# Attention products on 64-wide tiles of the TensorE array, a pair of heads at a time

## The chip, the cores and the metric

The kernel runs on one core of one Trainium2 chip. A core has a matrix engine (PE, with its weight loads listed apart as PEld), a vector engine (DVE), a scalar engine (ACT), GpSimd (POOL) and SyncE (SP, which here only issues DMAs); they run beside each other and wait for one another through semaphores. PE reads SBUF and writes only PSUM, which has eight banks. The metric is the device time of the whole program in microseconds.

## What is computed

A windowed attention feeds a feed-forward network; all inputs are float32 but for the two weight matrices, which are float64.

```python
B, H, S, D = (8, 8, 576, 64)
scores = q @ k.T / sqrt(D)
mask = (rel >= 0) & (rel < 64)        # rel = query position - key position
attn = softmax(where(mask, scores, -1e9))
x = (attn @ v) as [4608 tokens, 512]
h = x @ w_in                          # 512 -> 2048
sp = where(h > 20, h, log1p(exp(min(h, 20))))
out = (h * tanh(sp)) @ w_out          # 2048 -> 512
```

A query sees itself and the 63 tokens before it, so a block of 64 queries needs two blocks of 64 keys.

## The kernel before

**Tiling.** The 4608 tokens are taken in 12 chunks of 384 (CH), each of 6 blocks of 64 queries (NB). The 8 heads go in 4 pairs (NPAIR); the two heads of a pair fill the 128 partitions, 64 channels each.

**Attention of a chunk.** The work is cut into 8 units of (pair, group of three blocks). Each unit has three stages:

- `att_scores` (L109): for every block one product with 128 rows of contraction, 128 query columns and 128 key columns (L126). The query tile `q_t` comes from `q2`, which the host lays out so that a block has 128 columns, 64 for each head, with zeros in the rows of the other head; so one product gives the scores of both heads. VectorE then scales, masks and takes the row's extreme in one instruction a block (L131), ScalarE takes the exponential with a running sum (L135), VectorE adds 1e-9 and inverts (L137, L138), and the rows are multiplied by the inverse: for chunks 0 to 2 all on GpSimd, later two of three blocks on VectorE (L143) and one on GpSimd (L141).
- `att_transpose` (L146): for chunks 0 and 1 by PE into a PSUM bank and back by ScalarE (L157, L158); from chunk 2 on by 12 VectorE transposes of 32 by 32 squares a unit, over three blocks at a time (L153).
- `att_values` (L161): for every block one product of 128x128 with 128 columns (L165), of which the quarter for (head 0, head 0) and that for (head 1, head 1) are used; ScalarE casts each head's half to the float32r tile `xh` (L172) and VectorE writes the rest to `xl` (L173), two instructions each.

Every float32 product stands in the trace as two pairs of a weight load and a matmul, so 24 products a chunk for scores are 48 pairs, and as many for values.

**Feed-forward.** For each of 16 slices of 128 hidden columns, `ffn_in` (L175) makes h by 12 float32r products (high and low parts, L181), ScalarE, VectorE and GpSimd make the gate's tiles `gh` and `gl` (L188 to L200), and `ffn_out` (L206), two slices later, adds 9 products into three PSUM banks (L211). In stretches without attention beside them, `alone=True` copies h out of PSUM into a tile of the tag `pr` (L191, L192).

**Weights.** `load_w` (L225) splits the doubles into two float32r tiles, 32 pieces in all, four or five VectorE instructions each (L236 to L245), with a scratch tile `wa` of its own (two buffers).

**Order.** First the attention of chunks 0 and 1, with the first eight weight pieces placed behind marked units; then 24 slices of chunks 1 and 0 with two weight pieces after each until they are used up; then the last 8 slices of chunk 0 with the attention of chunk 2 beside them; then for each chunk c from 2 its 16 slices with the attention of chunk c + 1 beside them; the last chunk alone. `Att.plan` (L297) gives every stage a due time in half slices: units start `step` apart, the transpose `lat` later, the values 1.5 `lat` later. The order on each engine is then settled by the compiler's own scheduling within these priorities. The loads of q, k and v all go through SP's queue, two pairs ahead.

**PSUM.** Three banks for the sums (`ps_acc`), two for h (`ps_h`), three for attention (`ps_at`).

Of the kernel before, what the change touches and what calls it, by code (L numbers as in the profile page):

```python
# [11 lines left out]
F32 = mybir.dt.float32  # L12
# [7 lines left out]
BLK = 64          # the attention window; queries and keys go in blocks of it  # L20
# [3 lines left out]
WP = 512          # columns of weights taken at a time  # L24
# [3 lines left out]
def tile_window_attn_mish_ffn(  # L28
    ctx: ExitStack,
    tc: tile.TileContext,  # L30
    q2: bass.AP,      # [pairs, 128 (head of the pair, d), blocks x (head, 64 queries)], zero across heads
    kT: bass.AP,      # [pairs, 128, 64 + tokens]
    vN: bass.AP,      # [pairs, 64 + tokens, 128]
    w_in: bass.AP,    # [f tiles, 128, c tiles, 128], the doubles' bits
    w_out: bass.AP,   # [f tiles, 128, 512], the doubles' bits
    out: bass.AP,     # [tokens, 512]
# [3 lines left out]
    NPAIR, _, NT = q2.shape  # L40
    NT //= 2
# [6 lines left out]
    G = 3                       # blocks of an attention group  # L48
    NG = NB // G
# [16 lines left out]
    mask0 = const.tile([P, P], F32, name="mask0")  # L66
# [7 lines left out]
    nc.gpsimd.tensor_copy(mask0, mask)  # L74
    nc.gpsimd.memset(mask0[:, 0:BLK], NEG)

# [5 lines left out]
    pTs = [const.tile([P, G, P], F32, name=f"pT{i}") for i in range(2)]  # L82
# [4 lines left out]
    marks = {}        # the last of VectorE's instructions on a group's scores  # L87

    def load_qk(c, p):
        q_t = ap_.tile([P, NB, P], F32, name="q_t")  # L90
        k_t = ap_.tile([P, CH + BLK], F32, name="k_t", bufs=2)
        qf = q_t.rearrange("p n s -> p (n s)")
        parts = NG if c == 0 and p < 2 else 1
        for i in range(parts):
            a, b = i * CH // parts, (i + 1) * CH // parts
            nc.sync.dma_start(qf[:, 2 * a:2 * b], q2[p, :, 2 * (c * CH + a):2 * (c * CH + b)])
# [12 lines left out]
    def att_scores(c, i, tiles):  # L109
        p, g = units[i]  # L110
        q_t, k_t = tiles
        if c < 2:
            n = i % NTT
            s_ps = ps_acc.tile([P, G, P], F32, name="s_ps", tag=f"acc{n}")
        else:
            s_ps = ps_at.tile([P, G, P], F32, name="s_ps", tag="at")
        if c < 2 and i % 2 == 0:
            # the tiles of the gate, which has not begun
            pr = mp.tile([P, CH], F32, name="prt", tag="t", bufs=4).rearrange("p (g s) -> p g s", g=G)
        else:  # L120
            pr = ap_.tile([P, G, P], F32, name="pr", bufs=3)
        mx = ap_.tile([P, G], F32, name="mx", bufs=5)
        sm = ap_.tile([P, G], F32, name="sm", bufs=5)
        for j in range(G):
            n = g * G + j
            nc.tensor.matmul(s_ps[:, j, :], q_t[:, n, :], k_t[:, n * BLK:n * BLK + P],  # L126
                             start=True, stop=True)
        for j in range(G):
            first = (c * NB + g * G + j) % blocks_per_seq == 0
            # -(scores + mask) / 8 and its minimum, which is minus the maximum  # L130
            marks[c, i] = nc.vector.tensor_tensor_reduce(  # L131
                out=pr[:, j, :], in0=s_ps[:, j, :], in1=mask0 if first else mask,
                op0=ALU.add, op1=ALU.min, scale=-0.125, scalar=3.0e38, accum_out=mx[:, j:j + 1])
        for j in range(G):
            nc.scalar.activation(pr[:, j, :], pr[:, j, :], AF.Exp, bias=mx[:, j:j + 1], scale=-1.0,  # L135
                                 accum_out=sm[:, j:j + 1])
        nc.vector.tensor_scalar(sm, sm, 1e-9, None, ALU.add)  # L137
        nc.vector.reciprocal(sm, sm)  # L138
        for j in range(G):
            if c < 3 or j == G - 1:  # L140
                nc.gpsimd.tensor_scalar(pr[:, j, :], pr[:, j, :], sm[:, j:j + 1], 0.0, ALU.mult, ALU.add)  # L141
            else:
                nc.vector.tensor_scalar(pr[:, j, :], pr[:, j, :], sm[:, j:j + 1], None, ALU.mult)  # L143
        return pr

    def att_transpose(c, pr):  # L146
        pT = next(pTs)
        if c >= 2:
            # 32 by 32, without the squares that the mask empties
# [5 lines left out]
        t_ps = ps_h.tile([P, G, P], F32, name="t_ps", tag="h_ps")  # L155
        for j in range(G):
            nc.tensor.transpose(t_ps[:, j, :], pr[:, j, :], ident)  # L157
        nc.scalar.copy(pT, t_ps)  # L158
        return pT

    def att_values(p, g, v_t, pT, x):  # L161
        xh, xl = x
        o_ps = ps_at.tile([P, G, P], F32, name="o_ps", tag="at")
        for j in range(G):
            nc.tensor.matmul(o_ps[:, j, :], v_t[:, g * G + j, :], pT[:, j, :], start=True, stop=True)  # L165
        cols = slice(g * G * BLK, (g + 1) * G * BLK)
        for j in range(2):
            rows = slice(j * BLK, (j + 1) * BLK)
            src = o_ps[rows, :, rows]
            hi = xh[rows, p, cols].rearrange("p (n s) -> p n s", s=BLK)  # L170
            lo = xl[rows, p, cols].rearrange("p (n s) -> p n s", s=BLK)
            nc.scalar.copy(hi, src)  # L172
            nc.vector.tensor_tensor(lo, src, hi.bitcast(F32), ALU.subtract)  # L173

    def ffn_in(x, f, alone=False):  # L175
# [7 lines left out]
        t = mp.tile([P, CH], F32, name="t", bufs=4)  # L183
# [13 lines left out]
        # minus h * tanh(softplus(h)); the sign goes at the end  # L197
# [27 lines left out]
    def load_w(src, wh, wl):  # L225
        """Doubles [128, n] as the sum of two float32r tiles, by their bits."""
# [13 lines left out]
        # sign, 8 bits of exponent, 20 bits of the high word and 3 of the low one  # L240
# [18 lines left out]
    # attention of a chunk as a list of (pair, group), each in three stages  # L259
    units = [(p, g) for p in range(NPAIR) for g in range(NG)]  # L260
    NU = len(units)

    class Att:
# [18 lines left out]
        def scores(self, i):  # L282
            p, g = units[i]
            self.pr[i] = att_scores(self.c, i, self.qk[p])
# [130 lines left out]
```

## Time and profile before

| what | value |
|---|---|
| time, median of 3 runs | 1037.87 us (1037.74 to 1038.93) |
| the profiled execution: span of its instructions | 1039.1 us |
| PE busy / weight loads busy | 979.3 us (94%) / 877.7 us (84%) |
| DVE / ACT / POOL busy | 796.2 (77%) / 625.8 (60%) / 398.9 us (38%) |
| chain that ended last, by engine | PE 49%, DVE 34%, ACT 10% |
| HBM read / written | 65.54 / 9.44 MB |

The span is the time from the first to the last instruction of one execution, 1.2 us over the median of the timed runs. A matmul's end is modelled in the trace, so its busy time overlaps that of the next one; the distance from one start to the next is what a matmul costs in a row of them. "Idle before, releaser" names what an engine was waiting for.

### The profile page before, as it was taken

How to read it: one execution, taken by the hardware profiler on the slowest of the kernel's cores; microseconds unless marked ns; L12 is line 12 of the kernel's file. 1: busy time of each engine (PE TensorE's matmuls, PEld its weight loads, DVE VectorE, ACT ScalarE, POOL GpSimd, SP SyncE). 2: the span in 40 equal slices, each digit the busy share in tenths (PEclk: the TensorE clock that was granted, in tenths of full speed). 3: DMA queues.
4: the chain of work that ended last, by engine and by line, in shares of the span. 5: the costliest groups of instructions: out<-in, count | busy, mean ns of one | idle time of the engine just before them, and what ended most of it. 6: DMA issues, size and time to landing. Idle time of an engine off the chain costs nothing.

```text
span 1039.1 us, 16752 instructions
## 1 busy us (share of the span) xinstructions
PE 979.3 (94%) x5232; PEld 877.7 (84%) x5232; DVE 796.2 (77%) x2621; ACT 625.8 (60%) x1668; POOL 398.9 (38%) x583
## 2 busy tenths in 40 slices
PE   7689887977989999999999999999999999999998
PEld 6687776876979988898889898888988889888887
DVE  4899997798778778777787877877877887885332
ACT  6765776555656655665656565655665655655664
POOL 5645555432333332433334233343333333333432
PEclk9889999988999999999999999999999999999999
DMA  8743441232211211211311211221221211200000
GB/s 264 237 136 110 132 124 41 82 93 77 73 55 50 85 55 41 94 51 45 94 41 56 76 58 55 71 64 40 85 64 40 85 42 62 84 3 1 31 1 31
DMA packets 61913, 76.05 MB, mean 73 GB/s; under 512 B 3456, under 2 KB 47232, under 8 KB 61824
## 3 DMA queue, kind: packets, MB, share of 16 engines
q1 hardware_dynamic: 57936, 60.83, 18.8%
q0 software_dynamic: 3888, 14.16, 4.5%
q8 instruction: 41, 0.67, 0.3%
q14 instruction: 48, 0.39, 0.1%
HBM read 65.54 MB, written 9.44 MB: 72 GB/s over the span
## 4 chain that ended last, share of the span: by engine, by line
PE 49%; DVE 34%; ACT 10%; issue 4%; DMA 2%; POOL 1%; SPq 0%; ACTq 0%; DVEq 0%; POOLq 0%
PE h_ps L181 21%; PE acc L211 21%; DVE pT L153 13%; ACT pr L135 4%; PE o_ps L165 3%; PE s_ps L126 3%; DVE t L193 3%; DVE pr L143 3%; DVE t L198 2%; DVE wa L242 2%; DVE xl L173 2%; DVE sm L137 2%; DVE wa L243 2%; ACT t L194 1%; ACT t L195 1%
## 5 line engine op out<-in xcount | busy, mean ns | idle before, releaser
L199 POOL TENSOR_SCALAR gh<-t 128x384 fp32r<-128x384 f32 x192 | 104.1, 542 | 518.9 <-DVE t L198 374.9
L181 PE MATMUL h_ps<-xh,wi_h 128*128 128x384 f32 x768 | 275.3, 359 | 9.4 <-ACT h L192 7.4
L153 DVE STREAM_TRANSPOSE pT<-pr 32x96 f32<-32x96 f32 x960 | 258.4, 269 | 14.3 <-DVE pr L143 0.5
L181 PE MATMUL h_ps<-xl,wi_h 128*128 128x384 f32 x768 | 261.5, 340 | 1.5 <-DVE xl L173 1.4
L181 PE MATMUL h_ps<-xh,wi_l 128*128 128x384 f32 x768 | 260.9, 340 | 0.8 <-POOL wi_l L245 0.8
L194 ACT ACTIVATE t<-t 128x384 f32<-128x384 f32 x192 | 100.8, 525 | 232.3 <-DVE t L193 232.0
L211 PE MATMUL acc<-wo_h,gh 128*128 128x512 f32 x576 | 231.1, 401 | 5.5 <-POOL gh L199 5.5
L211 PE MATMUL acc<-wo_l,gh 128*128 128x512 f32 x576 | 228.0, 396 | 0.0
L211 PE MATMUL acc<-wo_h,gl 128*128 128x512 f32 x576 | 216.4, 396 | 0.0
L200 POOL TENSOR_TENSOR gl<-t,gh 128x384 fp32r<-128x384 f32 x192 | 199.9, 1041 | 15.6
L181 PEld LDWEIGHTS h_ps<-xh,wi_h 128*128 128x128 f32 x768 | 146.9, 191 | 17.9 <-ACT h L192 10.7
L181 PEld LDWEIGHTS h_ps<-xl,wi_h 128*128 128x128 f32 x768 | 147.2, 192 | 4.1 <-DVE xl L173 2.1
L181 PEld LDWEIGHTS h_ps<-xh,wi_l 128*128 128x128 f32 x768 | 146.5, 191 | 2.0 <-POOL wi_l L245 1.5
L198 DVE SCALAR_TENSOR_TENSOR t<-t,h_ps 128x384 f32<-128x384 f32 x152 | 83.8, 551 | 79.7 <-ACT t L196 77.4
L211 PEld LDWEIGHTS acc<-wo_h,gl 128*128 128x128 f32 x576 | 108.0, 188 | 26.6 <-POOL gl L200 1.0
L211 PEld LDWEIGHTS acc<-wo_h,gh 128*128 128x128 f32 x576 | 108.6, 189 | 25.8 <-POOL gh L199 8.3
L211 PEld LDWEIGHTS acc<-wo_l,gh 128*128 128x128 f32 x576 | 108.7, 189 | 17.6
L195 ACT ACTIVATE t<-t,half_b 128x384 f32<-128x384 f32 x192 | 118.3, 617 | 5.2
L135 ACT ACTIVATE pr<-pr,mx 128x128 f32<-128x128 f32 x264 | 102.6, 390 | 25.0 <-DVE mx L131 24.8
L165 PE MATMUL o_ps<-pT,v_t 128*128 128x128 f32 x576 | 92.4, 288 | 25.1 <-DVE pT L153 19.1
L193 DVE TENSOR_SCALAR t<-t 128x384 f32<-128x384 f32 x192 | 95.8, 500 | 25.5 <-ACT t L188 23.7
L165 PEld LDWEIGHTS o_ps<-pT,v_t 128*128 128x128 f32 x576 | 81.0, 198 | 39.1 <-DVE pT L153 18.5
(54 smaller groups left out, 1106.2 us busy)
## 6 DMA issues: line engine op xcount, KB each, us to landing
v_t<-vN SPq DMA_DIRECT2D x48, 384.0 KB, 3.5
q_t<-q SPq DMA_DIRECT2D x46, 384.0 KB, 3.3
k_t<-kT SPq DMA_DIRECT2D x46, 224.0 KB, 3.5
out<-o SPq DMA_DIRECT2D x36, 256.0 KB, 2.1
st<-w_out POOLq DMA_DIRECT2D x14, 512.0 KB, 4.0
st<-w_in POOLq DMA_DIRECT2D x13, 512.0 KB, 4.0
st<-w_in SPq DMA_DIRECT2D x3, 512.0 KB, 5.9
st<-w_out SPq DMA_DIRECT2D x2, 512.0 KB, 4.6
```

Source lines behind the costliest of these rows:

```text
L126: nc.tensor.matmul(s_ps[:, j, :], q_t[:, n, :], k_t[:, n * BLK:n * BLK + P], start=True, stop=True)
L135: nc.scalar.activation(pr[:, j, :], pr[:, j, :], AF.Exp, bias=mx[:, j:j + 1], scale=-1.0, accum_out=sm[:, j:j + 1])
L153: nc.vector.transpose(pT[k:k + 32, :, r:r + 32], pr[r:r + 32, :, k:k + 32])
L165: nc.tensor.matmul(o_ps[:, j, :], v_t[:, g * G + j, :], pT[:, j, :], start=True, stop=True)
L181: nc.tensor.matmul(h_ps, w[:, f, cc, :], xx[:, cc, :], start=n == 0, stop=n == 3 * NC_ - 1)
L193: nc.vector.tensor_scalar(t, t, EXP20, 1.0, ALU.min, ALU.add)
L194: nc.scalar.activation(t, t, AF.Square)
L195: nc.scalar.activation(t, t, AF.Ln, bias=half_b, scale=0.5)
L198: nc.vector.scalar_tensor_tensor(t, t, -1.0, h, ALU.add, ALU.mult)
L199: nc.gpsimd.tensor_scalar(gh, t, 1.0, 0.0, ALU.mult, ALU.add)
L200: nc.gpsimd.tensor_tensor(gl, t, gh.bitcast(F32), ALU.subtract)
L211: nc.tensor.matmul(acc[t], a[:, ts_], w[:, f, :], start=f == 0 and i == 0, stop=f == NF - 1 and i == 2)
```

## The change

The attention is written anew in units of a whole pair (six blocks), four units a chunk.

- **Scores.** `q_t` is the plain query layout, 384 columns in place of 768. Each block and head is a product of its own on a quarter of the array: 64 rows of contraction (the head's channels), 64 columns of queries, 128 key columns. The row half is the head, the column half the parity of the block, and the four quarters are visited in the order (0,0), (1,1), (1,0), (0,1) of (parity, head). Each head has its own PSUM bank. That is 48 products a chunk in place of 24.
- **Softmax.** VectorE's and ScalarE's instructions a block stay as many and as large; the sums are inverted six at a time; the multiplication by the inverse goes to GpSimd for all blocks.
- **Transposes.** From chunk 2 on still on VectorE, 12 a unit, now over six blocks at a time (32x192 in place of 32x96).
- **Values.** Each block and head is a product with 128 rows of contraction, 64 columns (the head's channels) and 64 query columns, on the left or right half of the array: 48 products a chunk in place of 24. The sums stand as x needs them, so one cast and one subtraction of 128x384 a pair take the place of four of 64x192 each.
- **Banks.** From chunk 2 on a unit takes two of the three attention banks for its scores and the third for its values; in chunks 0 and 1 every second pair takes the banks of the sums.
- **Around it.** `plan` spaces the four units by (slots - 2) / 5, transposes 0.6 of a step later, values a step later. The scratch tile `wa` now shares the four buffers of the gate's `t`; the tag `pr` has two buffers of six blocks in place of three of three blocks. The weight pieces stand behind the same pairs as before.

```diff
     def load_qk(c, p):
-        q_t = ap_.tile([P, NB, P], F32, name="q_t")
+        q_t = ap_.tile([P, CH], F32, name="q_t")
...
     def att_scores(...):
-        for j in range(G):
-            n = g * G + j
-            nc.tensor.matmul(s_ps[:, j, :], q_t[:, n, :], k_t[:, n * BLK:n * BLK + P],
-                             start=True, stop=True)
+        pr = ap_.tile([P, HM, P], F32, name="pr", bufs=2)
+        for m in range(NM):
+            for par, h in ((0, 0), (1, 1), (1, 0), (0, 1)):
+                n = 2 * m + par
+                rows = slice(h * BLK, (h + 1) * BLK)
+                nc.tensor.matmul(s_ps[h][par * BLK:(par + 1) * BLK, m, :],
+                                 q_t[rows, n * BLK:(n + 1) * BLK], k_t[rows, n * BLK:n * BLK + P],
+                                 start=True, stop=True)
...
-        for j in range(G):
-            if c < 3 or j == G - 1:
-                nc.gpsimd.tensor_scalar(pr[:, j, :], pr[:, j, :], sm[:, j:j + 1], 0.0, ALU.mult, ALU.add)
-            else:
-                nc.vector.tensor_scalar(pr[:, j, :], pr[:, j, :], sm[:, j:j + 1], None, ALU.mult)
+        for j in range(HM):
+            nc.gpsimd.tensor_scalar(pr[:, j, :], pr[:, j, :], sm[:, j:j + 1], 0.0, ALU.mult, ALU.add)
...
     def att_values(...):
-        for j in range(G):
-            nc.tensor.matmul(o_ps[:, j, :], v_t[:, g * G + j, :], pT[:, j, :], start=True, stop=True)
-        for j in range(2):
-            rows = slice(j * BLK, (j + 1) * BLK)
-            nc.scalar.copy(hi, src)
-            nc.vector.tensor_tensor(lo, src, hi.bitcast(F32), ALU.subtract)
+        for n in range(NB):
+            m, par = n // 2, n % 2
+            for h in range(2):
+                rows = slice(h * BLK, (h + 1) * BLK)
+                nc.tensor.matmul(o_ps[rows, n * BLK:(n + 1) * BLK], v_t[:, n, rows],
+                                 pT[:, h * NM + m, par * BLK:(par + 1) * BLK], start=True, stop=True)
+        nc.scalar.copy(xh[:, p, :], o_ps)
+        nc.vector.tensor_tensor(xl[:, p, :], o_ps, xh[:, p, :].bitcast(F32), ALU.subtract)
...
-            h = ap_.tile([P, CH], F32, name="h", tag="pr", bufs=3)
+            h = ap_.tile([P, CH], F32, name="h", tag="pr", bufs=2)
...
-        a = mp.tile([P, WP], U32, name="wa")
+        a = mp.tile([P, WP], U32, name="wa", tag="t", bufs=4)
...
-            step, lat = ((slots - 10) / NU, 2) if slots > 24 else ((slots - 3) / NU, 4)
+            step = (slots - 2) / (NPAIR + 1)
+            for p in range(NPAIR):
+                at = p * step
+                self.events += [(at, 2, self.scores, p), (at + 0.6 * step, 1, self.transpose, p),
+                                (at + step, 0, self.values, p)]
...
-    for u in (5, 9, 10, 11, 13, 15, 15, 15):
-        with tc.issue_after(marks[u // NU, u % NU].ins):
+    for u in (2, 4, 5, 5, 6, 7, 7, 7):
+        with tc.issue_after(marks[u // NPAIR, u % NPAIR].ins):
```

More of the change, by code (lines that the diff above doesn't have):

```diff
@@ L107, in load_v, with att_scores @@
         return v_t
[L109 to L110 removed]
+    def att_scores(c, p, tiles):
         q_t, k_t = tiles
[L112 to L136 removed]
@@ new lines, in att_scores @@
+        if c < 2 and p % 2 == 0:
+            s_ps = [ps_acc.tile([P, NM, P], F32, name="s_ps", tag=f"acc{h}") for h in range(2)]
+        else:
+            s_ps = [ps_at.tile([P, NM, P], F32, name="s_ps", tag="at") for h in range(2)]
+        pr = ap_.tile([P, HM, P], F32, name="pr", bufs=2)
+        mx = ap_.tile([P, HM], F32, name="mx", bufs=3)
+        sm = ap_.tile([P, HM], F32, name="sm", bufs=3)
+        for m in range(NM):
[5 more added lines that the diff above has]
+                                 start=True, stop=True)
@@ new lines, in att_scores @@
+        for m in range(NM):
+            first = [(c * NB + 2 * m + par) % blocks_per_seq == 0 for par in range(2)]
+            mk = firsts[first.index(True)] if any(first) else mask
+            for h in range(2):
+                j = h * NM + m
+                marks[c, p] = nc.vector.tensor_tensor_reduce(
+                    out=pr[:, j, :], in0=s_ps[h][:, m, :], in1=mk,
+                    op0=ALU.add, op1=ALU.min, scale=-0.125, scalar=3.0e38, accum_out=mx[:, j:j + 1])
+                nc.scalar.activation(pr[:, j, :], pr[:, j, :], AF.Exp, bias=mx[:, j:j + 1], scale=-1.0,
+                                     accum_out=sm[:, j:j + 1])
@@ L345, in tile_window_attn_mish_ffn @@
     ev = []
-    for u in range(2 * NU):
-        a, i = first[u // NU], u % NU
-        ev += [(u, 2, a.scores, i), (u + 1.5, 1, a.transpose, i), (u + 2.25, 0, a.values, i)]
+    for u in range(2 * NPAIR):
+        a, p = first[u // NPAIR], u % NPAIR
+        ev += [(u, 2, a.scores, p), (u + 0.75, 1, a.transpose, p), (u + 1.25, 0, a.values, p)]
     for _, _, fn, i in sorted(ev, key=lambda e: e[:2]):
```

82 lines of the change are left out of this document (34 added, 48 removed).

## The prediction

> **What bounds the kernel now.** I read the busy times first, then the chain of waits, then the span by stages, then one chunk from the steady part.
>
> ```profile
> PE 979.3 (94%) x5232; PEld 877.7 (84%) x5232; DVE 796.2 (77%) x2621; ACT 625.8 (60%) x1668; POOL 398.9 (38%) x583
> PE 49%; DVE 34%; ACT 10%; issue 4%; DMA 2%; POOL 1%; SPq 0%; ACTq 0%; DVEq 0%; POOLq 0%
> ```
>
> PE is busy nearly throughout, yet the chain stands on PE for only half the span and on VectorE for a third: the stages have different limits. The span cut where they change (time, then busy us of PE, PEld, DVE, ACT, POOL, then clock, DMA share, GB/s):
>
> ```profile
> 0.00:54.30 54.30, 38.55 (x239) 35.37 (x240) 36.42 (x181) 38.36 (x146) 30.99 (x72) 0.91 0.78 247
> 54.30:160.00 105.70, 92.95 (x438) 79.13 (x436) 104.88 (x169) 71.03 (x146) 57.53 (x66) 0.97 0.41 123
> 160.00:190.80 30.80, 26.80 (x126) 22.33 (x127) 20.54 (x28) 19.36 (x39) 17.53 (x19) 1.00 0.14 48
> 190.80:262.00 71.20, 59.11 (x322) 53.26 (x321) 62.33 (x264) 38.12 (x124) 23.14 (x45) 0.90 0.27 84
> 262.00:946.00 684.00, 673.47 (x3675) 608.76 (x3673) 542.91 (x1936) 405.80 (x1110) 235.42 (x339) 1.00 0.19 59
> 946.00:1039.10 93.10, 88.44 (x439) 78.82 (x438) 29.13 (x46) 53.14 (x105) 34.25 (x44) 0.99 0.05 18
> ```
>
> So: attention of chunks 0 and 1 to 54, where no engine is full; weights split to 160 with VectorE full (104.88 of 105.70); some feed-forward alone; the attention of chunk 2 beside eight slices from 191 to 262, with VectorE at 62.33 of 71.2 and PE waiting; then the steady part, PE at 98% (673.47 of 684) and VectorE at 79%; then the last chunk, without attention. From the chain in order of time (start, length), the same place in two successive chunks, and one slice of the last chunk:
>
> ```profile
> 516.79 2.23 PE h_ps L181 x12
> ...
> 596.74 2.25 PE h_ps L181 x12
> ...
> 958.87 2.08 PE h_ps L181 x12
> 960.95 2.10 PE acc L211 x9
> ```
>
> A chunk takes 596.74 - 516.79 = 79.95 us. Its 16 slices need 16 x (2.08 + 2.10) = 66.9 of PE, so the attention costs PE 13.0 a chunk. That difference, in the nine chunks 3 to 11, is what this change can move most.
>
> **What a product costs.** Merged rows of PE in order of time (start, length, form, count), and one chunk's groups by line (the columns are count, busy us, mean ns):
>
> ```profile
> 190.84 2.17 PE L126 MATMUL s_ps<-k_t,q_t 128*128 128x128 f32 x18
> 160.04 0.50 PE L211 MATMUL acc<-wo_h,gh 128*128 128x512 f32 x1 [1.90 <-POOL gh L199]
> 160.38 0.39 PE L211 MATMUL acc<-wo_l,gh 128*128 128x512 f32 x1
> 160.62 0.39 PE L211 MATMUL acc<-wo_h,gh 128*128 128x512 f32 x1
> L126 PE MATMUL s_ps<-k_t,q_t 128*128 128x128 f32 x48 | 7.9, 274 | 0.0
> L165 PE MATMUL o_ps<-pT,v_t 128*128 128x128 f32 x48 | 7.7, 282 | 0.9 <-DVE pT L153 0.9
> ```
>
> Eighteen scores matmuls last 2.17 with 0.274 for the last: (2.17 - 0.27) / 17 = 0.112 from one to the next. 96 of them are 10.7 of the 13.0; 2.3 are left for waits. After a stall the next matmul comes 0.34 later instead of 0.24, so a weight load of 128 columns that is not drawn ahead costs about 0.10. Load and product each being near 0.11, a pair of them at 0.112 is limited by both, which leaves open what half-sized ones do.
>
> **1. The pairs.** A chunk has 192 pairs in place of 96. Scores keep 128 key columns and halve the loaded columns; values halve both. No row shows a product on part of the array. Bounds: one after another, 96 x 0.112 + 96 x 0.056 = 16.1; everything beside everything, a quarter of 0.112 each, 192 x 0.028 = 5.4. I take 0.056 for both kinds: products on different quarters run beside each other, but weight loads come one after another, and one of 64 columns costs half of 0.10, rounded up to half a pair. 192 x 0.056 = 10.7, **no change**, within -5.3 and +5.4 a chunk.
>
> **2. Switching.** Today the step from feed-forward to attention and back is free: loads are drawn ahead across it. A change of the array's division may need it empty. Nothing here shows one; the bounds are nothing, and an exposed load plus the tail of a product, 0.10 + (0.27 - 0.11) = 0.26. Nearest is the restart above, at 0.10; I take 0.11, a whole pair's time. How often? PE's order breaks one chunk's attention into 28 runs of one kind, of which these are the first and the last:
>
> ```profile
> 520.96 0.38 PE L165 MATMUL o_ps<-pT,v_t 128*128 128x128 f32 x2
> ...
> 596.02 0.71 PE L165 MATMUL o_ps<-pT,v_t 128*128 128x128 f32 x4 [0.35 <-DVE pT L153]
> ```
>
> The new units are 8 runs if whole (4 of scores, 4 of values); I take 12, two changes each: 24 x 0.11 = **+2.6**, within 0 and 28 x 2 x 0.26 = 15.
>
> The Trainium skill (TensorEngine Tiling, Key Properties) says that changing the tiling mode drains TensorE. By its page TensorE: Matmul & The Clock Gate (Single matmul latency), the drain is some 0.175; 24 of those are, as an estimate, 4.2, and my total would be 14 us longer. No run here shows it yet.
>
> **3. VectorE, ScalarE, GpSimd.** Groups of the same chunk, and one row of twelve transposes:
>
> ```profile
> L153 DVE STREAM_TRANSPOSE pT<-pr 32x96 f32<-32x96 f32 x96 | 25.8, 269 | 1.3
> L198 DVE SCALAR_TENSOR_TENSOR t<-t,h_ps 128x384 f32<-128x384 f32 x16 | 8.8, 551 | 8.0 <-ACT t L196 7.7
> L143 DVE TENSOR_SCALAR pr<-pr,sm 128x128 f32<-128x128 f32 x16 | 7.6, 510 | 0.3
> L131 DVE CUSTOM_DVE_ANT_0 pr<-s_ps,mask 128x128 f32<-128x128 f32 x25 | 6.0, 287 | 0.5 <-PE s_ps L126 0.4
> L173 DVE TENSOR_TENSOR xl<-o_ps,xh 64x192 fp32r<-64x192 f32 x16 | 5.6, 353 | 2.3 <-ACT xh L172 2.0
> L137 DVE TENSOR_SCALAR sm<-sm 128x3 f32<-128x3 f32 x8 | 2.9, 364 | 3.5 <-ACT pr L135 3.5
> L135 ACT ACTIVATE pr<-pr,mx 128x128 f32<-128x128 f32 x24 | 9.3, 389 | 1.9 <-DVE mx L131 1.9
> L135 ACT ACTIVATION_READ_ACCUMULATOR pr<-pr,mx 128x1 f32 x24 | 4.5, 187 | 0.0
> L141 POOL TENSOR_SCALAR pr<-pr,sm 128x128 f32<-128x128 f32 x8 | 3.6, 446 | 0.8 <-DVE sm L138 0.8
> L200 POOL TENSOR_TENSOR gl<-t,gh 128x384 fp32r<-128x384 f32 x16 | 16.2, 1016 | 1.3
> 512.64 3.38 DVE L153 STREAM_TRANSPOSE pT<-pr 32x96 f32<-32x96 f32 x12
> ```
>
> Per chunk VectorE loses L143 whole (7.6), and of L173 all but four of 128x384 at L198's 0.551 (5.6 - 2.2 = 3.4), and half of L137 (1.5). Transposes: 96 at 3.38 / 12 = 0.28 become 48 twice as wide. From L131 to L198 256 more columns cost 0.264, so 96 more cost at least 0.10; bounds 0.38 and 0.56, I take the middle, 0.47: 27.0 - 22.6 = 4.4. Together 17 us less. But the steady part waits on VectorE only inside the 2.3 above: I credit **-0.5** (within -2.3 and +2). GpSimd gains 16 x 0.446 = 7.1 a chunk, 9% of 80 on 34%: hidden, with room.
>
> **4. Coarser units.** A pair's chain: six exponentials with their readings, 6 x (0.389 + 0.187) = 3.5; six GpSimd multiplications, 2.7, behind a `gl` of 1.0; twelve transposes, 5.6. That is 12.8. The plan gives 6 half slices, 6 x 80 / 32 = 15. It fits with 2 to spare, so nothing for it here; the rival below prices its failing.
>
> Steady part: (0 + 2.6 - 0.5) x 9 = **+19**, rounded.
>
> **5. Chunk 2's attention (191 to 262).** VectorE was the limit there, with this wait on it:
>
> ```profile
> PE o_ps L165 <- DVE pT L153: 8.7, 3, 4.6
> ```
>
> PE waited 8.7 us for transposes, in three waits. VectorE sheds what part 3 lists but L143 (GpSimd did that already), 9.3; the switches give 2.6 back: **-6**, within -12 and +4.
>
> **6. Start (to 54).** Loads are on the chain, and q's halve (issue, count, size, us to landing; then chain rows):
>
> ```profile
> q_t<-q SPq DMA_DIRECT2D x8, 384.0 KB, 4.6
> 23.29 4.93 DMA k_t<-kT
> 38.61 7.42 DMA v_t<-vN
> ```
>
> Eight of 192 KB less are 1.5 MB, at the stage's 247 GB/s 6 us of DMA time; I credit half, because pairs go two deep where groups went three deep: **-3**, within -8 and +6. The loads keep their order on SP's queue; none is moved past another.
>
> **7. Weights (54 to 160).** VectorE has no slack there, and its instructions stay. But `wa` now shares four buffers with `t`, so a piece can wait until the `gl` of an earlier slice has read its `t`. If each of the 24 later pieces waited one `gl` (1.016), that would be 24 us; two pieces a slice come slowly, so I take an eighth: **+3**, within 0 and 12. That h has two `pr` tiles in place of three I cost at nothing: two slices take 2 x 4.18 = 8.4 us at the fastest, and h is held from one to the next; if that cover is gone, ScalarE's copy waits for VectorE, as `wa` does.
>
> Sum: 19 - 6 - 3 + 3 = +13. The profiled span is 1039.1 and the median 1037.87; the sum is put on the median: **1051**.
>
> **The rivals.** *Everything runs side by side* (the faster side): loads of different quarters overlap too, so pairs cost 0.028, 5.4 a chunk. It decides from where pairs cost under 0.048: 192 x 0.008 = 1.5 a chunk then pays for the rest of the sum. Per chunk -5.3 + 2.6 - 0.5 = -3.2, times 9 = -29, with -6: **1003**. For it: each quarter has its own rows and columns. Against: today's loads never come closer than 0.11 in a row of them. The Trainium skill (TensorEngine Tiling, Key Properties) backs it: different tiles can load weights and multiply in parallel. Chance 0.33.
>
> *Switching is free*: as I sum it, without part 2: 9 x -0.5 - 6 = **1027**. For it: today's fp32 and fp32r matmuls follow each other without loss. Chance 0.07.
>
> *Nothing overlaps*: the change doesn't do what it says; 16.1 a chunk: (5.4 + 2.1) x 9 - 6 = +61, **1099**. Chance 0.14.
>
> *The coarse unit comes late*: PE waits for pT before each pair's values. The wait above was 8.7 / 3 = 2.9; a third of it in 36 pairs of nine chunks is 36 us: 1051 + 36 = **1087**. It decides where the chain of part 4 exceeds 15 us. For: GpSimd and VectorE run other work between its links. Against: VectorE is 17 us lighter. Chance 0.10.
>
> **How the numbers follow.** My forecast has 0.36. Its own range, from 1035 to 1066, has the switches and the small terms at half their ways; its end below 1040, about 0.07, is no change (0.2%, or 2 us, is what a measurement of this kernel can tell), a sliver faster. Faster: 0.33 + 0.07 + 0.01 = 0.41. Same: 0.06. Slower: 0.29 + 0.14 + 0.10 = 0.53. The range from 990 (side by side, switches at 1.1) to 1090 leaves out the better end of the first rival, and most of the third.
>
> **What would show it.** Scores and values pairs at 0.056 in rows of the changed trace, against 0.028 or 0.112; a gap of 0.1 or more where feed-forward meets attention; wide transposes near 0.47; a PE wait for pT in each pair if the units come late; the chunk's period at 82 against 77 or 87. A period under 79 makes my forecast wrong.

## The result and the profile after

The changed kernel takes 1055.47 us (median of 4 runs, 1055.12 to 1056.4) against 1038.34 us (4 runs), a ratio of 1.0162 (95% interval 1.0147 to 1.0176): **slower by 1.6%**. Its profiled span is 1053.3 us, 14.2 more than before. The forecast of 1051 was near, but most of its terms were wrong; that their errors cancelled is luck.

From the page of the changed kernel, the busy times, the shares of the chain, and the group of the wide transposes:

```profile
PE 978.7 (93%) x6384; PEld 831.0 (79%) x6384; DVE 590.1 (56%) x1757; ACT 595.5 (57%) x1524; POOL 449.5 (43%) x729
PE 78%; DVE 10%; ACT 3%; POOL 3%; issue 2%; DMA 2%; SPq 0%; ACTq 0%; POOLq 0%; DVEq 0%
L152 DVE STREAM_TRANSPOSE pT<-pr 32x192 f32<-32x192 f32 x480 | 177.5, 370 | 58.7 <-POOL pr L142 51.8
```

VectorE's load falls by 206 us, and its share of the chain from 34% to 10%. Read alone, this looks like a gain. The windows of the changed kernel, cut where those of before were cut (time, then busy us of PE, PEld, DVE, ACT, POOL, then clock, DMA share, GB/s), show where it went:

```profile
0.00:54.30 54.30, 32.12 (x374) 23.01 (x375) 26.63 (x140) 29.63 (x115) 26.33 (x66) 0.81 0.60 192
54.30:160.00 105.70, 74.73 (x330) 61.87 (x329) 95.75 (x163) 58.38 (x119) 55.89 (x62) 0.84 0.42 139
...
190.80:262.00 71.20, 63.94 (x444) 54.21 (x442) 37.67 (x126) 39.04 (x107) 28.46 (x50) 1.00 0.20 64
262.00:946.00 684.00, 677.35 (x4581) 576.20 (x4581) 378.48 (x1236) 389.69 (x1021) 285.51 (x484) 0.99 0.16 52
```

The last row is the steady part, with PE still full (677 of 684). In the row above it VectorE has 37.7 where it had 62.3: it no longer limits chunk 2's attention. In the first, PE and VectorE get less done than before (32.1 and 26.6 against 38.6 and 36.4). In the second VectorE had been full (104.88 of 105.7) and is now idle for 10 us, although its work there was not made smaller; PE did 330 matmuls where it had done 438. Part of that is the start, which now reaches into this window; the rest is a new wait. For a sum by stages I take the start of ScalarE's first exponential of h in the slice that opens each stage, first in the kernel before, then in the changed one:

```profile
60.70 0.49 ACT L188 ACTIVATE t<-h_ps 128x384 f32<-128x384 f32 x1 [0.82 <-PE h_ps L181]
166.76 0.49 ACT L188 ACTIVATE t<-h_ps 128x384 f32<-128x384 f32 x1 [0.19 <-PE h_ps L181]
242.80 0.49 ACT L188 ACTIVATE t<-h_ps 128x384 f32<-128x384 f32 x1
965.24 0.49 ACT L188 ACTIVATE t<-h_ps 128x384 f32<-128x384 f32 x1 [0.94 <-PE h_ps L181]
```

```profile
72.16 0.49 ACT L189 ACTIVATE t<-h_ps 128x384 f32<-128x384 f32 x1 [2.42 <-PE h_ps L182]
199.29 0.49 ACT L189 ACTIVATE t<-h_ps 128x384 f32<-128x384 f32 x1 [1.03 <-PE h_ps L182]
269.29 0.49 ACT L189 ACTIVATE t<-h_ps 128x384 f32<-128x384 f32 x1 [1.30 <-PE h_ps L182]
977.61 0.49 ACT L189 ACTIVATE t<-h_ps 128x384 f32<-128x384 f32 x1 [1.56 <-PE h_ps L182]
```

| stage, from mark to mark | before | after | difference | predicted |
|---|---|---|---|---|
| start, to the first slice's exponential | 60.7 | 72.2 | +11.5 | -3 |
| weights: the next 22 slices | 106.1 | 127.1 | +21.0 | +3 |
| to chunk 2's first exponential (its attention) | 76.0 | 70.0 | -6.0 | -6 |
| to chunk 11's first exponential (nine chunks' attention) | 722.4 | 708.3 | -14.1 | +19 |
| to the end | 73.9 | 75.7 | +1.8 | 0 |
| span | 1039.1 | 1053.3 | +14.2 | +13 |

So the steady part, which the forecast made slower, is faster; the loss lies in two stages that it had put at three microseconds each. The same place in two chunks of the chain of waits of the changed kernel:

```profile
517.43 2.29 PE acc L212 x9
...
596.16 2.29 PE acc L212 x9
```

A chunk takes 596.16 - 517.43 = 78.7 us in place of 79.95. Merged rows of PE just before (start, length, form, count) show what the products and the changes between them cost:

```profile
507.06 0.40 PE L212 MATMUL acc<-wo_h,gh 128*128 128x512 f32 x1
507.29 0.40 PE L212 MATMUL acc<-wo_l,gh 128*128 128x512 f32 x1
507.62 0.34 PE L171 MATMUL o_ps<-pT,v_t 128*64 128x64 f32 x4
...
509.16 0.80 PE L171 MATMUL o_ps<-pT,v_t 128*64 128x64 f32 x20
509.89 0.65 PE L125 MATMUL s_ps<-k_t,q_t 64*64 64x128 f32 x12
510.47 0.44 PE L182 MATMUL h_ps<-xh,wi_h 128*128 128x384 f32 x1
510.75 0.34 PE L182 MATMUL h_ps<-xl,wi_h 128*128 128x384 f32 x1
510.93 0.34 PE L182 MATMUL h_ps<-xh,wi_l 128*128 128x384 f32 x1
```

*The pairs.* Twenty values matmuls last 0.80; with 0.23 for the last (its mean in this chunk's groups) that is 0.57 / 19 = 0.030 from one to the next. The single records show how: two products on different column halves start 0.007 apart, and the next two 0.058 later; four scores products on the four quarters start 0.006 to 0.007 apart, and the next four 0.109 later; the weight loads stand as close. So a scores pair costs 0.109 / 4 = 0.027 and a values pair 0.058 / 2 = 0.029, and a chunk's attention 96 x 0.027 + 96 x 0.029 = 5.4 in place of 10.7.

*The changes.* Between two sums of the feed-forward lie 0.23 us (507.06, 507.29), but 0.33 to the first values product (507.62); after the last scores product the second h comes 0.28 after the first (510.47, 510.75), the third 0.18 later. By the single records going into attention costs 0.14 and coming out 0.20. PE's order has 20 runs of attention of one kind a chunk and 31 changes, as some runs touch: 31 x 0.17 = 5.3. The sum is 66.9 + 5.4 + 5.3 = 77.6; about 1 us of the 78.7 stays unassigned.

*The waits.* So products and changes cancel, and the steady part is faster by something else. PE's waits from chunk 2's first exponential to chunk 11's (total, times, longest), in the kernel before and then in the changed one:

```profile
PE o_ps L165 <- DVE pT L153: 15.0, 24, 4.6
```

```profile
PE o_ps L171 <- issue: 3.2, 1, 3.2
PE o_ps L171 <- DVE pT L152: 0.7, 1, 0.7
```

The waits for VectorE's transposes are gone: 15.0 us have become 3.9 in all, 11 of the 14.1. About half of them, 7.9, stood in the first of the nine chunks, whose period falls from 86.4 to 80.9; in a middle chunk it was 0.9 in three waits, and is none now. Whether VectorE's lighter work or the new spacing of the units took them away no run separates.

### The profile page after: what moved, and what is told of

Read it like the earlier page. It is cut to its first block, busy times and chain, and to the rows that moved or that the text cites. A ratio compares the mean times of both kernels' runs of the same rounds, so it can differ in the third digit from the quotient of the medians.

```text
span 1053.3 us, 18054 instructions
## 1 busy us (share of the span) xinstructions
PE 978.7 (93%) x6384; PEld 831.0 (79%) x6384; DVE 590.1 (56%) x1757; ACT 595.5 (57%) x1524; POOL 449.5 (43%) x729
## 4 chain that ended last, share of the span: by engine, by line
PE 78%; DVE 10%; ACT 3%; POOL 3%; issue 2%; DMA 2%; SPq 0%; ACTq 0%; POOLq 0%; DVEq 0%
PE h_ps L182 35%; PE acc L212 34%; PE s_ps L125 5%; PE o_ps L171 4%; DVE pT L152 2%; POOL pr L142 2%; ACT pr L137 2%; DVE wa L243 1%; DMA st<-w_out 1%; DVE wa L244 1%; DVE wa L240 1%; DVE wa L242 1%; DVE pr L134 1%; POOL gh L200 1%; DVE t L194 1%
## 5 line engine op out<-in xcount | busy, mean ns | idle before, releaser
L182 PE MATMUL h_ps<-xh,wi_h 128*128 128x384 f32 x768 | 269.5, 351 | 8.7 <-ACT h L193 5.8
L200 POOL TENSOR_SCALAR gh<-t 128x384 fp32r<-128x384 f32 x192 | 108.4, 565 | 389.8 <-DVE t L199 377.9
L212 PE MATMUL acc<-wo_h,gh 128*128 128x512 f32 x576 | 235.4, 409 | 22.3 <-POOL gh L200 22.2
L152 DVE STREAM_TRANSPOSE pT<-pr 32x192 f32<-32x192 f32 x480 | 177.5, 370 | 58.7 <-POOL pr L142 51.8
L201 POOL TENSOR_TENSOR gl<-t,gh 128x384 fp32r<-128x384 f32 x192 | 196.3, 1022 | 15.8
L212 PE MATMUL acc<-wo_h,gl 128*128 128x512 f32 x576 | 201.9, 399 | 0.0
L189 ACT ACTIVATE t<-h_ps 128x384 f32<-128x384 f32 x192 | 93.8, 489 | 178.3 <-PE h_ps L182 152.9
L142 POOL TENSOR_SCALAR pr<-pr,sm 128x128 f32<-128x128 f32 x288 | 109.9, 401 | 132.4 <-DVE sm L140 130.3
L137 ACT ACTIVATE pr<-pr,mx 128x128 f32<-128x128 f32 x288 | 111.7, 389 | 24.8 <-DVE mx L134 22.8
```

Source lines behind the costliest of these rows:

```text
L152: nc.vector.transpose(pT[k:k + 32, :, r:r + 32], pr[r:r + 32, :, k:k + 32])
L182: nc.tensor.matmul(h_ps, w[:, f, cc, :], xx[:, cc, :], start=n == 0, stop=n == 3 * NC_ - 1)
L200: nc.gpsimd.tensor_scalar(gh, t, 1.0, 0.0, ALU.mult, ALU.add)
L201: nc.gpsimd.tensor_tensor(gl, t, gh.bitcast(F32), ALU.subtract)
L212: nc.tensor.matmul(acc[t], a[:, ts_], w[:, f, :], start=f == 0 and i == 0, stop=f == NF - 1 and i == 2)
```

## The experiments

Each ratio is taken against runs of the kernel before that were made beside it. "First exponential", "weights" (the 22 slices after it) and "chunk" (period) are measured as above.

### The ring of the scratch tile

**The ring alone, in the kernel before.**

```diff
-        a = mp.tile([P, WP], U32, name="wa")
+        a = mp.tile([P, WP], U32, name="wa", tag="t", bufs=4)
```

> The kernel before with one line of the change alone: the weights' scratch tile wa shares the four buffers of the gate's t. If the shared ring is what cost the weights' stage (21 us between the first and the last split piece in the changed kernel), this is slower than before by 12 to 21 us, about 1050 to 1059, with VectorE idle in the stage and ScalarE's first step on a piece waiting for gl. If the ring is harmless and the stage was late for other reasons (coarse units, two tiles for h), it stays within 3 us of before.

Measured: 1064.39 us, ratio 1.0248 (1.0226 to 1.027). First exponential 59.7, weights 134.0 in place of 106.1, chunk 80.0. The new ring alone costs 28 us of the weights, with the old attention. The windows of this kernel, the second stage:

```profile
54.30:160.00 105.70, 71.76 (x274) 59.52 (x275) 98.18 (x168) 59.86 (x115) 54.50 (x56) 0.82 0.40 130
```

VectorE again falls short of full (98.18), and PE does 274 matmuls.

**The rings apart, in the changed kernel.** The scratch tile has its two buffers back; the room comes from one buffer of `t` and from `ident`, which goes into a buffer of `gh`.

```diff
-    ident = const.tile([P, P], F32, name="ident")
+    ident = mp.tile([P, P], F32, name="ident", tag="gh", bufs=3)
-        t = mp.tile([P, CH], F32, name="t", tag="t", bufs=4)
+        t = mp.tile([P, CH], F32, name="t", tag="t", bufs=3)
-        a = mp.tile([P, WP], U32, name="wa", tag="t", bufs=4)
+        a = mp.tile([P, WP], U32, name="wa")
```

> The changed kernel with the ring undone: wa has two buffers of its own again, t has three (there is no room for four), the identity matrix stands in a gh buffer. If the ring is the cause, 10 to 20 us come back: 1036 to 1045. If it is not, 1055, or more, because t has one buffer less.

Measured: 1034.41 us, ratio 0.997 (0.9956 to 0.9984): 21 us less than the changed kernel, and a little under the kernel before. Weights 111.5 in place of 127.1, first exponential 69.6, chunk 78.7.

```profile
54.30:160.00 105.70, 91.48 (x462) 78.25 (x460) 99.54 (x172) 69.85 (x148) 63.80 (x69) 0.94 0.38 129
```

The two runs agree: the ring is most of the loss of the weights' stage, 15.6 of its 21.0 in the changed kernel. The mechanism stands in the chain of waits of the changed kernel, in which ScalarE's part of a weight piece twice follows the last reader of an older `t`:

```profile
119.65 1.06 POOL gl L201
...
120.73 0.69 ACT wa L239
121.42 0.42 ACT t L195
...
129.21 1.01 POOL gl L201
...
130.24 0.68 ACT wa L239
130.92 0.42 ACT t L195
```

The piece's first write to `wa` (here on ScalarE, for the earlier pieces on VectorE) starts 0.02 after GpSimd's `gl` has ended, since `gl` was the last to read that buffer as `t`. Behind it stand the rest of the piece on VectorE and, next on ScalarE, the gate of the slice at hand (`t`, 121.42), whose own `gl` then lets go of the next buffer late. In the waits of the changed kernel from 60 to 200 us this shows on other names:

```profile
PEld acc L212 <- POOL gh L200: 23.9, 9, 4.4
POOL st L230 <- DVE wa L244: 18.7, 7, 9.1
```

PE waits for gates and GpSimd, which issues the pieces' loads, for earlier pieces; in the kernel before the same two rows have 4.6 and 11.2 us (60 to 167 us). The wait for the ring itself (`ACT wa L239 <- POOL gl L201`) has only 3.4 us in two waits. The list names what came last, not what made it late; so how 3.4 us of waits grow to 21 is argued here and not shown. The granted clock falls as well, 0.84 and, with the ring in the kernel before, 0.82, against 0.97 (third column from the right): PE idles more, and what part of the loss is the clock's no run separates. Of the stage, 5.4 us stay lost with the rings apart; whether the one buffer fewer of `t` does it was not tried, since a fourth finds no room. With half units (below) and the same three buffers the stage takes 106.8, but the next one is then 3.5 longer.

### What the steady part gains

**One quarter three times in a row.** The same 48 products, but all three of a quarter before the next quarter.

```diff
-        for m in range(NM):
-            for par, h in ((0, 0), (1, 1), (1, 0), (0, 1)):
+        for par, h in ((0, 0), (1, 1), (1, 0), (0, 1)):
+            for m in range(NM):
```

> The changed kernel, but the scores' products visit one quarter of the array three times before the next. If products are cheap because different quarters run beside each other (four in 0.109 us in the changed kernel's trace), those on the same quarter follow at about 0.109 each: 96 pairs a chunk at up to 0.109 in place of 0.027 are +6 to +8 us a chunk, so 1110 to 1130. If they are cheap because half-sized loads and products are, whatever quarter they use, this is 1055 within 5.

Measured: 1103.17 us, ratio 1.0626 (1.0604 to 1.0647); chunk 83.3. Against the changed kernel a chunk is 4.6 longer from the order of the products alone. Rows of PE of this kernel:

```profile
517.88 0.86 PE L125 MATMUL s_ps<-k_t,q_t 64*64 64x128 f32 x6
518.68 0.45 PE L182 MATMUL h_ps<-xh,wi_h 128*128 128x384 f32 x1
```

Six matmuls on one quarter last 0.86, less some 0.29 for the last: 0.11 from one to the next, as a full 128x128 pair before. A quarter is no faster than the whole array; the gain comes only from the others beside it. The loss is less than expected because PE draws the last product of one quarter beside the first of the next, 0.055 apart in the single records. Of the 4.6, some 0.7 are four more changes a chunk (35 in place of 31).

**Whole runs.** Can the changes be had for less? Values of the odd blocks first, so that none can begin before the last transposes, and VectorE reads the blocks in reverse, so that the next unit's scores come in one run.

```diff
-        for m in range(NM):
+        for m in reversed(range(NM)):
...
-        for n in range(NB):
+        for n in (1, 3, 5, 0, 2, 4):
```

> The changed kernel with two loops in another order, so that the products of a unit are not parted by feed-forward work: values take the odd blocks first (they wait for all transposes anyway), and VectorE reads the last written block of scores first. PE then changes between feed-forward, scores and values 20 times a chunk in place of 31. If a change costs 0.17 to 0.19 us, the chunk's period falls by 1.9 to 2.1 from 78.7, and the whole by 17 to 19: about 1037. If what is left over the products' own time is waiting and not changing, it stays at 1055 within 4.

Measured: 1061.29 us, ratio 1.0218 (1.0195 to 1.0241), 6 us more than the changed kernel. The changes did go from 31 to 20 a chunk, but the period only from 78.7 to 78.3, in place of the 11 x 0.17 = 1.9 that they are worth, and the attention of chunk 2 became 6 us longer. PE's waits in one chunk of this kernel:

```profile
PE h_ps L182 <- DVE t L199: 1.4, 1, 1.4
```

In the changed kernel PE waits for nothing there. A block of transposes with the gate's `t` behind it on VectorE stands in both, in the changed kernel and then in this one:

```profile
502.60 4.22 DVE L152 STREAM_TRANSPOSE pT<-pr 32x192 f32<-32x192 f32 x11
```

```profile
491.44 4.20 DVE L152 STREAM_TRANSPOSE pT<-pr 32x192 f32<-32x192 f32 x11
```

In the changed kernel PE comes to its next h at 510.47, when `t` is done (509.55 and 0.55); here, with fewer changes ahead of it, it comes 1.4 sooner than it can start, and waits until 498.97 for a `t` that ends at 498.91. With the values' order alone, on top of the kernel with half units below:

> The kernel of e6 with values taking the odd blocks first, and nothing else: 20 changes a chunk in place of 31, and scores read by VectorE in the old order. If changes cost 0.17 to 0.19 and the wait for VectorE that came with the reversed reading is gone, 1.9 to 2.1 us a chunk come off: 17 us under e6, about 1011. If PE waits instead, as with the reversed reading, 0 to 4 us under e6.

Measured: 1035.4 us, ratio 0.995 (0.9929 to 0.9971), against 0.9936 without it: nothing gained. 20 changes, chunk 78.3, chunk 2 5.7 later, and the same wait:

```profile
PE h_ps L215 <- DVE t L232: 1.6, 2, 1.4
```

So the changes have a price, but here those removed come back as waits: by these rows some of them had stood where PE would else have waited for VectorE.

**Values alone.** The kernel before with only its values products on column halves, in its own units of three blocks.

```diff
-            nc.tensor.matmul(o_ps[:, j, :], v_t[:, g * G + j, :], pT[:, j, :], start=True, stop=True)
+            for h in range(2):
+                rows = slice(h * BLK, (h + 1) * BLK)
+                nc.tensor.matmul(o_ps[rows, j * BLK:(j + 1) * BLK], v_t[:, g * G + j, rows],
+                                 pT[:, j, rows], start=True, stop=True)
```

> The kernel before with one part of the change alone: values on half the array's columns, in the old units of three blocks. Pairs side by side save 48 x 0.111 - 96 x 0.029 = 2.5 us a chunk. But values now stand apart from all else: some 15 runs a chunk, entered and left, 30 changes. If a change costs 0.17 to 0.19, that is 5.1 to 5.7, so 2.6 to 3.2 us a chunk more: about 1065. If changes cost nothing and the rest was waiting, 2.5 less a chunk: about 1013.

Measured: 1048.73 us, ratio 1.0092 (1.0066 to 1.0119); chunk 81.8, 1.8 longer. The products save 48 x 0.112 - 96 x 0.029 = 2.6, so the 34 changes into and out of values runs cost 4.4 net. The 0.9 that PE waited for transposes in a chunk before are gone here too (PE waits for nothing in the middle chunks); with them the changes cost 5.3, 0.16 each. Were changes free, the chunk would be 77.4 at most. Switching is not free, and with short runs it costs more than the tiling gains. In the start this kernel is early (first exponential 55.8), so it is not the values' new form that is late there. Nor does an early start count in full: 4.9 us ahead at the first slice, this kernel reaches the 22nd slice after it at 167.55, where the kernel before does at 166.76. The rows of the table add up to the span, but a microsecond in one of them is not always one of the total.

### The start

With the rings apart the first exponential still comes at 69.6 in place of 60.7. I take the end of the last values of the two first chunks too: 55.3 before (the row's start and length), 66.8 with the rings apart.

```profile
54.51 0.83 PE L165 MATMUL o_ps<-pT,v_t 128*128 128x128 f32 x6
```

**Half units in the softmax.** Chunks 0 and 1 with two tiles of three blocks a pair, each with its own sums and multiplications, one of them in a buffer of `t`; otherwise the rings apart.

```diff
+        if c < 2:
+            return halves(c, p, s_ps, q_t, k_t)
...
+        for h in range(2):
+            ...
+            for m in range(NM):
+                nc.gpsimd.tensor_scalar(pr[:, m, :], pr[:, m, :], sm[:, m:m + 1], 0.0, ALU.mult, ALU.add)
```

> The changed kernel with the rings apart (1034.4) and, in chunks 0 and 1 alone, the softmax in half units: one head's three slots at a time, each with its own tile, sums and transposes, so that five half tiles are in flight in place of two whole ones. If the start was late (the first slice's exponential at 69.6 us against 60.7 before) because whole units wait for two tiles, 5 to 9 us come back: 1025 to 1030. If it was late for another reason (the loads, the switches on PE), it stays at 1034 within 3.

Measured: 1033.23 us, ratio 0.9936 (0.9914 to 0.9959); first exponential 69.7. The size of the softmax's unit alone is not what makes the start late; that theory falls. The depth is not what it was, though: five half tiles (three buffers of `t`, two of `pr`), where the kernel before has seven (four and three).

**The pieces behind the sums.** The early weight pieces queue behind a pair's reciprocal.

```diff
-                marks[c, p] = nc.vector.tensor_tensor_reduce(
+                nc.vector.tensor_tensor_reduce(
...
-        nc.vector.reciprocal(sm, sm)
+        marks[c, p] = nc.vector.reciprocal(sm, sm)
```

> The kernel with separate rings, with each early weight piece placed behind a pair's reciprocal in place of behind its last score instruction, so that its four or five VectorE instructions queue behind the inverse that GpSimd's multiplications wait for, and not ahead of it. Theory (pieces standing ahead of the inverses make the start late; GpSimd waited 9.2 us for the inverses there): the first slice's exponential comes 5 to 8 us before the 69.6 of separate rings and the time is 1027 to 1030. Rival (the start is set by loads and by the lower granted clock): the exponential within 2 us of 69.6 and the time 1033 to 1036. Period 78.7 by both.

Measured: 1031.2 us, ratio 0.9924 (0.9902 to 0.9946); first exponential 69.7, last values at 64.8. The place of the pieces among the sums is not it either; GpSimd's wait for the sums in the first 72 us rose from 9.2 to 22.6, and the start was no later for it.

**All pieces last**, in the changed kernel with the rings apart, with half units besides, and in the kernel before (there the last of its sixteen half units, 15, eight times):

```diff
-    for u in (2, 4, 5, 5, 6, 7, 7, 7):
+    for u in (7, 7, 7, 7, 7, 7, 7, 7):
```

> The kernel with separate rings, with all eight early weight pieces placed behind the last pair of the two first chunks, so that none of them stands among the first seven pairs' work on VectorE. This isolates the attention of the two first chunks: where the pieces make the start late, the values of the fourth and the eighth pair come at least 8 us earlier than with separate rings; where loads and clock set it, they come within 3 us of it. The first slice's exponential itself may come later by up to 15 us, since eight pieces of about 2 us then stand in one row before it; time 1034 to 1050. Period 78.7 by both.

> The kernel with the softmax of the two first chunks in half units, and all eight early weight pieces placed behind the last pair. With whole units and the pieces last the fifth pair's values begin at 44.0 and the eighth's end at 59.7, 4.4 us after those of before. Theory (coarse units cost the start what the pieces don't): the last values end by 57 and the first slice's exponential comes at 60 to 62.5. Rival (the units' size costs the start nothing, what is left is the lower granted clock): last values at 58.5 to 60.5, exponential at 63.5 to 66. Time 1040 to 1050 by both, since the pieces come late.

> The kernel before, with only its eight early weight pieces placed behind the last unit of the two first chunks. In the changed kernel with separate rings this brought the last values from 66.8 to 59.7. Theory (half units keep three tiles in flight and hide the pieces; only the coarse units expose them): the last values, at 55.3 in the kernel before, end within 2 us of that. Rival (the pieces cost the start of either kernel the same): they end 5 us or more earlier, by 50. Time 1040 to 1060 by both, since the pieces come late.

Measured: 1047.09 us, ratio 1.0067 (1.0047 to 1.0087), first exponential 64.9; 1052.38 us, ratio 1.0115 (1.0085 to 1.0145), 68.6; 1048.18 us, ratio 1.0087 (1.007 to 1.0104), 57.3. The last values of the two first chunks (start, length), one row each for the rings apart, the pieces last, the same with half units, and the kernel before with the pieces last:

```profile
65.85 0.91 PE L171 MATMUL o_ps<-pT,v_t 128*64 128x64 f32 x22
```

```profile
58.17 1.54 PE L171 MATMUL o_ps<-pT,v_t 128*64 128x64 f32 x22
```

```profile
59.23 1.54 PE L204 MATMUL o_ps<-pT,v_t 128*64 128x64 f32 x22
```

```profile
49.32 1.50 PE L165 MATMUL o_ps<-pT,v_t 128*128 128x128 f32 x12
```

The pieces cost the changed kernel 66.8 - 59.7 = 7.1 and the kernel before 55.3 - 50.8 = 4.5: both pay for them, the coarse units 2.6 more. Without pieces in the way, 59.7 - 50.8 = 8.9 are left, and half units don't take them (60.8): both theories that made the size of the softmax's unit the cause miss.

**The next pair's scores ahead.** The order of the stages in the two first chunks was changed with the units: transposes came 1.5 half units after the scores, so behind the next unit's scores; 0.75 of a pair puts them ahead. Put back, on top of the pieces behind the sums:

```diff
-        ev += [(u, 2, a.scores, p), (u + 0.75, 1, a.transpose, p), (u + 1.25, 0, a.values, p)]
+        ev += [(u, 2, a.scores, p), (u + 1.1, 1, a.transpose, p), (u + 1.6, 0, a.values, p)]
```

> The kernel with separate rings and the marks behind the sums, with one more edit: in the two first chunks a pair's transposes are due 1.1 pairs after its scores in place of 0.75, and its values 1.6 in place of 1.25, so that the scores of the next pair stand ahead of them on PE. (In the kernel before the transposes came 1.5 half units after the scores, hence also behind the next unit's scores.) Theory (PE takes its instructions in order, so the next pair's scores wait behind transposes that wait for GpSimd, and the pairs go one after another): the eighth pair's values end by 60 in place of 64.8 and the first slice's exponential comes at 62 to 66 in place of 69.7; time 1023 to 1028. Rival (GpSimd and the weight pieces set the pace of the pairs whatever PE's order): values' end and exponential within 2 us of 64.8 and 69.7, time 1029 to 1033. Period 78.7 by both.

Measured: **1030.13 us, ratio 0.992 (0.9906 to 0.9933)**, the lowest median of all kernels here, though not clear of the one before it (0.9924). First exponential 67.6, last values at 63.6: 2.1 and 1.2 earlier than there, at most a quarter of what was left. The order on PE is a small part.

*What stays open* is some 7 us of the start. Two readings fit and were not tried. The first is the loads: PE's waits for keys in the first 60 us (total, times, longest), in the kernel before and then with the rings apart:

```profile
PE s_ps L126 <- DMA k_t<-kT: 6.6, 5, 3.6
```

```profile
PE s_ps L125 <- DMA k_t<-kT: 14.8, 6, 3.4
```

They grew by 8.2; on SP's queue two loads of weights stand ahead of the third pair's queries, where one stood. Against this, the third pair's values end hardly later than before (27.5 and 27.0). For it, with the pieces last in both kernels PE waits 14.6 for keys against 6.5, and the second pair's values already end 6.2 later (26.6 against 20.4), most of the 8.9; but no run moved a load. The second is the granted clock: from 20 to 40 us 0.71 with the rings apart and 0.84 before. Against this, the kernel before with the pieces last ran at 0.76 from 40 to 60 and was early. Untried too are the banks, which the rewrite shares out anew in these two chunks (the kernel before put all their scores into the banks of the sums), and the depth of seven half tiles.

## Why the number held and the steps did not

**The pairs (0 of the steady part): wrong.** The step took 0.056, because "weight loads come one after another". They do not, on different quarters: 0.027 and 0.029, the lower bound, so -5.3 a chunk. This is the mechanism of the first rival. The rule beside it, from the Trainium skill (TensorEngine Tiling (Array Packing), Key Properties: different tiles load weights and multiply in parallel), agrees with the trace: 0.007 between two starts. Today's loads at 0.11 spoke of one tile only, and I let them speak of four.

**Switching (+2.6): right in kind, too small in both factors.** 31 changes in place of 24, at 0.17 in place of 0.11: 5.3. The drain that the Trainium skill states in the same section agrees with the trace too: the estimate of 0.175 from TensorE: Matmul & The Clock Gate (Single matmul latency), which is stated there for bf16, lies between the 0.14 and 0.20 measured. I had preferred a row that measures something else, a restart after a stall.

**VectorE's relief (-0.5): too small, within its bounds.** PE's waits for transposes in the steady part fell from 15.0 us to 0.7, 1.6 a chunk; with the 3.2 of the other wait it is 1.2. The step saw that the waits on VectorE lie inside the 2.3, and credited a quarter of them; most went, by the lighter VectorE or by the new spacing. The wide transposes took 0.370, just under the lower bound given.

**Steady part: +19 forecast, -14.1 measured.** The text said that a period under 79 makes the forecast wrong; it is 78.7. The first rival's -29 had the right pairs but the same cheap changes. By the measured prices pairs and changes cancel (-5.3 + 5.3); what is left is the waits for VectorE's transposes that went, as told above: in a middle chunk the 2.3 us beside products and changes became about 1, and 5.5 of the 14.1 come from the first of the nine chunks alone.

**Coarser units in the steady part: right.** PE waits for `pT` once there, 0.7 us. **Chunk 2: -6, right**, through the transposes as argued (PE's waits for them were 8.7 from 190 to 262 us, and are two of together 1.6 in the changed kernel); with the rings apart the stage gains 8.

**Start (-3): wrong sign, +11.5.** The step counted bytes, and took the start for a stream of loads. The bytes fell and the start was late all the same; the share of the pieces and of the order is told above, and for some 7 us the cause stays open.

**Weights (+3, within 0 and 12): the mechanism right, the size a seventh.** The step named the wait (`gl` must have read its `t`) and priced the full case at 24 us, then took an eighth, because "two pieces a slice come slowly". The stage was full on VectorE; a stall in it has no slack to hide in, and +21 came, near the whole case. That it is near is no proof of that sum: one `gl` a piece is not what the trace shows (the ring's own waits are 3.4 us in two), and the ring alone cost 28. But the window had the warning, an engine with 0.8 us of slack in 105.7.

So the total came near because an error of -33 in the steady part (+19 to -14.1) met +14.5 in the start, +18 in the weights and +1.8 at the end. (A slip besides: the fourth rival's 36 pairs at a third of 2.9 us are 35, not 36.)

## What to carry to other kernels

Tiles of the array gain from neighbours: let successive products visit different tiles, and keep runs of one division long, as each change has a price (here 0.14 to 0.20 us); but look first whether PE would only wait for another engine in its place. A change of buffers that comes along with a change of arithmetic is a change of its own: look at which stage each shared ring runs in, and be slow to discount a wait in a stage whose engine is full. Undo such riders first; here three lines turned a loss of 1.6% into a gain of 0.3%, and two small edits of order made it 0.8%.

## What the runs showed of the hardware

- Matmuls of 64x128 on the four quarters started 0.006 to 0.007 us apart and four took 0.109, as one matmul of 128x128 did (0.112); on one quarter each took 0.11.
- Loads and products of the two column halves ran side by side although both use all 128 rows: 0.058 for two.
- A change between the whole array and its parts cost 0.14 going in and 0.20 coming out, 0.16 on average where only values were split (from the chunk's period and the waits that went).
- VectorE's transposes of 32x192 took 0.370, those of 32x96 0.269 to 0.28: twice the columns for 1.35 times the time.
